# Last expert of a mixture-of-experts layer: weight conversions, the seventh expert's turns, a row gather and its sums each in an earlier step

## The chip, the cores and the metric

One core of a Trainium2 chip runs the whole program. The metric is the time of one execution on the device in microseconds (us). The engines are TensorE (PE), VectorE (DVE), ScalarE (ACT), GpSimd (POOL) and SyncE (SP). Each works through its own queue of instructions and waits on semaphores for the others. DMA transfers are issued here by SP (weights), ACT (rows of results) and POOL (gathers by index).

## What is computed

Attention with a local window, then a mixture of experts with the two best of eight experts per token, then a dense layer with the mish function. Only the second is around the change, and the first lines of the third.

```python
def _moe_ref(x, w_gate, w_noise, noise, w1, w2):
    ...
    for e in range(E):                       # 8 experts
        for k in range(2):
            mask = top2[:, k] == e
            h = np.maximum(x[mask] @ w1[e], 0.0)       # 512 -> 1024
            out[mask] += top2_w[mask, k, None] * (h @ w2[e])   # 1024 -> 512

def _moe2_ref(x, w_in, w_out):
    h = x @ w_in                             # 512 -> 2048
    sp = np.where(h > 20.0, h, np.log1p(np.exp(np.minimum(h, 20.0))))
    return ((h * np.tanh(sp)) @ w_out).astype(np.float32)
```

## The kernel before, in words

Every float32 product is made of three products of split operands (`three`, lines 858 to 860): high times high, high times low, low times high. So each operand exists as a high part, written by ACT, and a low part, written by DVE as the difference.

The experts run in 64 steps, `n = 8 * e + f`, with expert `e` and a block `f` of 128 of the 1024 hidden units. Each expert has up to 416 tokens (`CAP`). In a step:

- `first_layer(e, f)` makes 12 matmuls into a bank `hp`; ACT writes `hhi` (L904) and DVE `hlo` (L905) from it.
- `whole_layer` of the step before makes the second layer of the previous block, 12 matmuls from `hhi` and `hlo` into four banks `ac`. Its second matmul reads `hlo`.
- `w_split` splits the piece of expert weights that is needed two steps later: ACT writes `whi` (L277), DVE `wlo` (L280). `w_load` issues a load of 512 KB on SP (L265).
- In some steps `w64_begin` begins a conversion for the third layer, whose weights arrive as 64-bit words: four operations on DVE (L327 to L330). The last operations of a conversion, `half[4]`, stand in the next step: one on ACT (L322) and two on DVE (L323, L324). Below, "begin f" and "end f" are these two parts of the conversion that begins in step `f` of the last expert. `CONVS` lists the steps. `w64_load` issues the load of such a piece (512 KB, L301). All these loads share three buffers (`raw`), and a load waits until DVE has read the buffer's last content.
- In steps 1 to 4 of an expert, `turn_out` turns a quarter of the previous expert's result on PE (L934), ACT copies it to `ys` (L940) and stores it in `yd` (L941).

In the last expert (`e = 7`, steps `n` 56 to 63) there is more. `rest_rows` gathers six times 128 rows from `yd` on POOL (L1009), where the stores of all earlier experts have to be in; `rest_sum` weighs and adds each pair, on ACT (L1016) and DVE (L1017). Then comes `finish`: three quarters of the last block's second layer; `rest_turn`, which turns the sums on PE (L1024); copies of the four quarters of the result to `yT`, on ACT (L1038) and DVE (L1036); turns of these (L1043), the fourth quarter, and products that put the last expert's rows in their places (L1052). The third layer follows on PE.

The order of all this is the order in which the Python code issues it. On each engine the instructions stand in that order.

Of the kernel before, what the change touches and what calls it, by code (L numbers as in the profile page):

```python
# [20 lines left out]
NTOK, DM, E, F1, F2 = 1536, 512, 8, 1024, 2048  # L21
# [26 lines left out]
WEIGH = (3, 7)  # L48
ROOM = 2 * P + 3 * 2 * 32
CONV = (1, 3, 5)  # L50
CONVS = [8 * e + f for e in range(8) for f in CONV]
CONVS[0] = 7


# [122 lines left out]
def build(tc, ctx, I, out, n_global, n_local, dbg=None):  # L177
# [126 lines left out]
    def w64_begin():  # L304


        j, s = divmod(state["conv"], 2)
        if j == 16:
            return None
        state["conv"] += 1  # L310
        if s == 0:
            pool, n = (wlast, "l") if j < 16 - RING else (wring, "")
            pieces[64 + j] = (pool.tile([P, 1024], F32R, name="whi" + n), pool.tile([P, 1024], F32R, name="wlo" + n))
        raw = raws.pop((j, s))
        lw, uw = raw[:, :, 0], raw[:, :, 1]
        hi, lo = (w[:, s * 512:(s + 1) * 512] for w in pieces[64 + j])
        t1 = wtmp.tile([P, 512], I32, name="t1", bufs=2)
        t2 = wtmp.tile([P, 512], I32, name="t2", bufs=1)
        f1 = t1.bitcast(F32)

        def rest():
            A.activation(hi, f1, AF.Copy)  # L322
            V.tensor_tensor(f1, f1, hi.bitcast(F32), op=OP.subtract)  # L323
            V.tensor_tensor(lo, f1, lo.bitcast(F32), op=OP.add)  # L324

        return (
            lambda: V.tensor_scalar(t1, uw, 0x07FFFFFF, 3, op0=OP.bitwise_and, op1=OP.logical_shift_left),  # L327
            lambda: V.scalar_tensor_tensor(t1, uw, -0x40000000, t1, op0=OP.bitwise_and, op1=OP.bitwise_or),
            lambda: V.tensor_scalar(t2, t1, -0x800000, None, op0=OP.bitwise_and),
            lambda: V.scalar_tensor_tensor(lo, lw.bitcast(U32), 2.0 ** -52, t2.bitcast(F32), op0=OP.mult, op1=OP.mult),  # L330
            rest,
        )
# [3 lines left out]
    def gather(e, blocks=NT):  # L336
        for c, n in CHUNKS:
            k = e * 4 + c // P
            idx = (gidx if blocks == NT else gidx0)[:n, k:k + 1]
            xg = xg_p.tile([P, DM], F32, name="xg")  # L340
            G.indirect_dma_start(out=xg[:n], out_offset=None, in_=xd[:1 + blocks * P],
                                 in_offset=bass.IndirectOffsetOnAxis(ap=idx, axis=0))
            xgs[e, c] = xg
# [510 lines left out]
    ps_q = ctx.enter_context(tc.tile_pool(name="ps_q", bufs=1, space=PSUM))  # L854
# [30 lines left out]
    def turn_in(e, ci, pool, name):  # L885
        c, n = CHUNKS[ci]
        if ci == 0:
            xgT[e] = parts()
        xg = xgs.pop((e, c))
        tp = pool.tile([P, 4, P], F32, name=name)  # L890
        for d in range(4):
            T.transpose(tp[:, d, :n], xg[:n, d * P:(d + 1) * P], ident[:n, :n])  # L892
        split_ps(xgT[e][0][:, :, c:c + n], xgT[e][1][:, :, c:c + n], tp[:, :, :n])

    def first_layer(e, f):
        whi, wlo = (w.rearrange("p (d f) -> p d f", d=4) for w in pieces[8 * e + f // 2 * 2])
        xhi, xlo = xgT[e]
        c = (f % 2) * P
        hp = ps_h.tile([P, 512], F32, name="hp")
        for d in range(4):  # L900
            three(hp[:, :CAP], whi[:, d, c:c + P], wlo[:, d, c:c + P], xhi[:, d], xlo[:, d], d == 0, d == 3)
        hhi = mk.tile([P, CAP], F32R, name="hhi")
        hlo = mk.tile([P, CAP], F32R, name="hlo")
        A.activation(hhi, hp[:, :CAP], AF.Relu)  # L904
        V.scalar_tensor_tensor(hlo, hp[:, :CAP], 0.0, hhi.bitcast(F32), op0=OP.max, op1=OP.subtract)  # L905
        hT[e, f] = (hhi, hlo)
# [12 lines left out]
    def whole_layer(e, f):  # L919
        for _ in second_layer(e, f):  # L920
            pass
        if f == 7:
            yT[e] = mk.tile([P, 4, CAP], F32, name="yT", bufs=1)
            for d in range(4):
                if d % 2:
                    V.tensor_copy(yT[e][:, d], yps[e][d][:, :CAP])
                else:
                    A.activation(yT[e][:, d], yps[e][d][:, :CAP], AF.Copy)

    def turn_out(e, ci, pool, name):  # L930
        c, n = CHUNKS[ci]
        tp = pool.tile([P, 4, P], F32, name=name)
        for d in range(4):
            T.transpose(tp[:n, d], yT[e][:, d, c:c + n], ident)  # L934
        store_y(e, ci, tp)

    def store_y(e, ci, tp):
        c, n = CHUNKS[ci]
        ys = mk.tile([P, DM], F32, name="ys", bufs=3)
        A.activation(ys[:n], tp[:n].rearrange("p a b -> p (a b)"), AF.Copy)  # L940
        (nc.scalar if e + 1 < E else nc.sync).dma_start(yd[e * CAP + c:e * CAP + c + n, :], ys[:n])  # L941

    def some_places(t, n, name):

        ohr, ohc, ops = places_of(t, n, wlast.tile([P, 1024], F32R, name=name).bitcast(F32))
        for op in ops:
            op()
        return ohr, ohc

    def whole_list(parts):  # L950
        list_of(parts, ps_q.tile([P, 4, P], F32, name="tq").rearrange("p a b -> p (a b)")[:, :64])
# [36 lines left out]
    def places():  # L988

        oh = mk.tile([P, DM], F32, name="ys", bufs=3).rearrange("p (t s) -> p t s", s=P)  # L990
        for t in range(TC):
            V.tensor_scalar(oh[:, t], iot[:, :P], chi[:, t:t + 1], None, op0=OP.is_equal)
        ps = ps_q.tile([P, TC + 1, P], F32, name="tq")
        for t in range(TC):
            T.transpose(ps[:, t], oh[:, t], ident)
        for t in range(TC):
            T.matmul(ps[:, TC, :1], oh[:, t], wlh[:, 1, t:t + 1], start=(t == 0), stop=(t == TC - 1))
        V.tensor_copy(place, ps[:, :TC])
        V.tensor_copy(wslot, ps[:, TC, :1])

    def rest_rows():

        rl, rh = parts()
        got = []
        for t in range(TC):
            r = []
            for k, (w, idx) in enumerate(((rl, cidx[:, 0, t:t + 1]), (rh, crest[:, t:t + 1]))):
                y = w.rearrange("p a b -> p (a b)")[:, t * DM:(t + 1) * DM].bitcast(F32)
                G.indirect_dma_start(out=y, out_offset=None, in_=yd[:(E - 1) * CAP, :],  # L1009
                                     in_offset=bass.IndirectOffsetOnAxis(ap=idx, axis=0))  # L1010
                r.append(y)
            got.append(r)
        return got

    def rest_sum(t, r):
        A.activation(r[0], r[0], AF.Copy, scale=wlh[:, 0, t:t + 1])  # L1016
        V.scalar_tensor_tensor(r[1], r[1], wrest[:, t:t + 1], r[0], op0=OP.mult, op1=OP.add)  # L1017
# [80 lines left out]
    half = None  # L1098
    for n, (e, f) in enumerate(steps):
        if f == 0 and 0 < e < E - 1:  # L1100
            gather(e + 1)
        first_layer(e, f)
        if early and n < len(PARTS):
            lists.append(some_places(*PARTS[n]))
        if n == 1 and not early:
            gather(1)
        if 2 <= f <= 4 and e:
            turn_out(e - 1, f - 1, ps_q, "tq")
        if n == 7:
            turn_in(1, 3, ps_q, "tq")  # L1110
        if n:
            whole_layer(*steps[n - 1])
        if f == 1 and e:
            turn_out(e - 1, 0, ps_q, "tq")
        if n == LISTS and early:
            whole_list(lists)
            gather(1)
        if n == WEIGH[0]:
            weigh()
        if n == WEIGH[1]:  # L1120
            places()
        if (e, f) == (E - 1, 5):
            rest = rest_rows()
        if (e, f) == (E - 1, 7):
            for t in range(TC):
                rest_sum(t, rest[t])
        for ci in range(3 if e == 0 else 4):
            if f == (TURN if e == 0 else (3, 4, 5, 6))[ci] and e + 1 < E:
                turn_in(e + 1, ci, ps_q, "tq")
        conv = n in CONVS if n < 61 else True  # L1130

        if n + 1 in CONVS if n < 60 else True:
            w64_load()
        if n:
            w_split(A, V)
            w_load()
        if half:
            half[4]()
        half = w64_begin() if conv else None
        if half:  # L1140
            for op in half[:4]:
                op()
    half[4]()
    late = finish(rest)
    if "y" in dbg:
        nc.sync.dma_start(dbg["y"], yd[:7 * CAP])
# [99 lines left out]
    for n in range(len(steps) + 2):  # L1246
        new, old = n < len(steps), 1 <= n <= len(steps)
        if new:
            tb, f = steps[n]
# [3 lines left out]
        if n % 2 == 0:  # L1253
            half = w64_begin() if n else None
# [145 lines left out]
```

## Time and profile before

| | |
|---|---|
| median of 3 runs | 736.98 us (736.25 to 737.54) |
| the profiled execution | 739.06 us, of which 737.2 us from the first to the last instruction |
| PE busy | 708.8 us (96%) |
| DVE busy | 523.9 us (71%) |
| ACT busy | 424.0 us (58%) |
| mean granted TensorE clock | 0.986 of full speed |

The profiled execution took 2.1 us more than the median of the runs, 0.3%. The times within the trace are counted from the first instruction. The last expert's steps lie at about 390 to 428 us, `finish` at 428 to 442 us, and the third layer behind it.

### The profile page before, as it was taken

What the parts mean: (1) busy time and instruction counts of PE and PEld (TensorE: products, weight loads), DVE (VectorE), ACT (ScalarE), POOL (GpSimd) and SP (SyncE); (2) the same over time, 40 slices, a digit from 0 to 9 for tenths busy, and PEclk for the clock granted to TensorE, in tenths of its full rate; (3) what the DMA queues carried; (4) which work ended last, traced back from release to release, by engine and by line L of the source; (5) the groups of instructions that cost most, each with busy time, mean ns of one, the idle gap of its engine ahead of it and who ended that gap; (6) DMA issues with size and microseconds to landing.
All of it is one profiled execution on the core that took longest, in us unless ns stands there. A gap on an engine that the chain in (4) does not pass through costs nothing.

```text
span 737.2 us, 11732 instructions
## 1 busy us (share of the span) xinstructions
PE 708.8 (96%) x4259; PEld 643.7 (87%) x4259; DVE 523.9 (71%) x1237; ACT 424.0 (58%) x892; POOL 61.6 (8%) x83
## 2 busy tenths in 40 slices
PE   8999899999999999999999989898999999999995
PEld 4777779999999999999999978787999989989993
DVE  7789769977586676758575876888666666666663
ACT  5899632444444544444444437566667667667663
POOL 2000200301010100101000212100120020000000
PEclk9999899999999999999999999999999999999998
DMA  7799321757475655647454734300120030001001
GB/s 166 217 220 240 127 67 39 244 159 232 161 221 167 198 186 177 221 158 219 151 170 142 236 106 135 112 29 0 56 74 1 0 106 10 0 1 44 1 0 47
DMA packets 42932, 89.26 MB, mean 121 GB/s; under 512 B 5987, under 2 KB 18403, under 8 KB 42868
## 3 DMA queue, kind: packets, MB, share of 16 engines
q1 hardware_dynamic: 35412, 69.37, 31.4%
q0 software_dynamic: 4096, 13.11, 5.9%
q10 hardware_dynamic: 3360, 5.97, 2.1%
q8 instruction: 35, 0.57, 0.3%
q14 instruction: 29, 0.24, 0.1%
HBM read 75.32 MB, written 13.11 MB: 120 GB/s over the span
## 4 chain that ended last, share of the span: by engine, by line
PE 79%; DVE 10%; ACT 6%; DMA 2%; issue 1%; POOL 1%; ACTq 0%; DVEq 0%
PE hp L858 11%; PE hp L859 11%; PE hp L860 11%; PE ac L858 6%; PE ac L860 6%; PE ac L859 6%; PE ac L1225 5%; PE ac L1226 5%; PE ac L1230 4%; PE xp L567 3%; PE tp L554 2%; PE sp L516 2%; PE tq L892 2%; PE tq L934 2%; ACT r L1187 1%
## 5 line engine op out<-in xcount | busy, mean ns | idle before, releaser
L858 PE MATMUL hp<-xgh,whi 128*128 128x416 f32 (+1 forms) x288 | 104.2, 362 | 0.0
L280 DVE TENSOR_TENSOR wlo<-raw,whi 128x1024 fp32r<-128x1024 f32 x61 | 74.6, 1223 | 38.1 <-ACT whi L277 35.9
L859 PE MATMUL hp<-xgl,whi 128*128 128x416 f32 (+1 forms) x288 | 100.6, 349 | 0.2 <-DVE xgl L711 0.2
L860 PE MATMUL hp<-xgh,wlo 128*128 128x416 f32 (+1 forms) x288 | 100.7, 350 | 0.0
L858 PE MATMUL ac<-hhi,whi 128*128 128x416 f32 x256 | 92.0, 359 | 0.0
L859 PE MATMUL ac<-hlo,whi 128*128 128x416 f32 x256 | 90.1, 352 | 0.3 <-DVE hlo L905 0.3
L860 PE MATMUL ac<-hhi,wlo 128*128 128x416 f32 x256 | 90.1, 352 | 0.0
L1196 DVE SCALAR_TENSOR_TENSOR yT<-yT,r 128x384 f32<-128x384 f32 (+1 forms) x68 | 36.4, 535 | 73.9 <-ACT r L1191 69.9
L858 PE MATMUL hp<-xgh,whil 128*128 128x384 f32 x224 | 77.0, 344 | 0.0
L859 PE MATMUL hp<-xgl,whil 128*128 128x384 f32 x224 | 76.4, 341 | 0.0
L904 ACT ACTIVATE hhi<-hp 128x416 fp32r<-128x416 f32 x64 | 33.3, 520 | 74.7 <-PE hp L860 64.6
L860 PE MATMUL hp<-xgh,wlol 128*128 128x384 f32 x224 | 75.9, 339 | 0.0
L277 ACT ACTIVATE whi<-raw 128x1024 fp32r<-128x1024 f32 x61 | 64.4, 1055 | 17.2 <-PE ac L859 12.0
L1225 PE MATMUL ac<-whil,hhi 128*128 128x512 f32 x144 | 57.3, 398 | 1.5 <-ACT hhi L1201 1.3
L1226 PE MATMUL ac<-wlol,hhi 128*128 128x512 f32 x144 | 56.6, 393 | 0.0
L859 PEld LDWEIGHTS hp<-xgl,whi 128*128 128x128 f32 x288 | 54.3, 189 | 1.1 <-DVE xgl L711 0.4
L858 PEld LDWEIGHTS hp<-xgh,whi 128*128 128x128 f32 x288 | 54.2, 188 | 1.1 <-ACT xgh L710 0.4
L1181 ACT ACTIVATE yT<-hp 128x384 f32<-128x384 f32 (+1 forms) x68 | 31.6, 471 | 40.6 <-PE hp L860 37.4
L860 PEld LDWEIGHTS hp<-xgh,wlo 128*128 128x128 f32 x288 | 54.0, 188 | 0.4
L863 ACT ACTIVATE xgh<-tq 128x512 fp32r<-128x512 f32 (+2 forms) x38 | 20.2, 533 | 57.8 <-PE tq L892 57.8
L1201 ACT ACTIVATE hhi<-yT 128x384 fp32r<-128x384 f32 (+1 forms) x68 | 34.5, 507 | 31.7 <-DVE yT L1198 30.7
L905 DVE SCALAR_TENSOR_TENSOR hlo<-hp,hhi 128x416 fp32r<-128x416 f32 x64 | 37.5, 586 | 16.7 <-ACT hhi L904 16.7
(241 smaller groups left out, 1526.2 us busy)
## 6 DMA issues: line engine op xcount, KB each, us to landing
raw<-in_w_moe SPq DMA_DIRECT2D x96, 512.0 KB
yd<-ys ACTq DMA_DIRECT2D x21, 256.0 KB
ks<-in_k_t SPq DMA_DIRECT2D x24, 136.0 KB
qr<-in_q_t SPq DMA_DIRECT2D x24, 128.0 KB
vt<-in_v_w SPq DMA_DIRECT2D x12, 256.0 KB
xd<-xs SPq DMA_DIRECT2D x12, 256.0 KB
out<-ys SPq DMA_DIRECT2D x12, 256.0 KB
vt<-in_v_w SPq DMA_DIRECT2D x10, 208.0 KB
```

What stands on the lines that cost most here:

```text
L277: A.activation(hi, raw, AF.Copy)
L280: e_lo.tensor_tensor(lo, raw, hi.bitcast(F32), op=OP.subtract)
L858: T.matmul(ps, whi, xhi, start=first, stop=False)
L859: T.matmul(ps, whi, xlo, start=False, stop=False)
L860: T.matmul(ps, wlo, xhi, start=False, stop=last)
L904: A.activation(hhi, hp[:, :CAP], AF.Relu)
L905: V.scalar_tensor_tensor(hlo, hp[:, :CAP], 0.0, hhi.bitcast(F32), op0=OP.max, op1=OP.subtract)
L1181: A.activation(m[1][:, cc], m[0][:, cc], AF.Exp)
L1196: V.scalar_tensor_tensor(s, s, 1.0, r, op0=OP.add, op1=OP.mult)
L1201: A.activation(g[0][:, cc], m[1][:, cc], AF.Copy)
L1225: T.matmul(acc2[tb][c], ghi[:, cc], whi, start=(f == 0), stop=False)
L1226: T.matmul(acc2[tb][c], ghi[:, cc], wlo, start=False, stop=False)
```

## The change

The last expert's conversions begin in steps f = 1, 3, 4, 5, 6 instead of 1, 3, 5, 6, 7; nothing of a conversion is then left for after the last step. Their loads are issued a step earlier from the third of them on. The seventh expert's four turns stand in steps 1, 2, 3 and 3 (behind the second layer) instead of 1, 2, 3 and 4. The gathers stand in step 4 instead of 5 and the sums in step 6 instead of 7. The numbers of instructions stay the same.

```diff
-CONVS = [8 * e + f for e in range(8) for f in CONV]
+CONVS = [8 * e + f for e in range(7) for f in CONV] + [57, 59, 60, 61, 62]
...
-        if 2 <= f <= 4 and e:
+        if 2 <= f <= 4 and 0 < e < E - 1 or (e, f) == (E - 1, 2):
             turn_out(e - 1, f - 1, ps_q, "tq")
+        if (e, f) == (E - 1, 3):
+            turn_out(e - 1, 2, ps_q, "tq")
...
         if f == 1 and e:
             turn_out(e - 1, 0, ps_q, "tq")
+        if (e, f) == (E - 1, 3):
+            turn_out(e - 1, 3, ps_q, "tq")
...
-        if (e, f) == (E - 1, 5):
+        if (e, f) == (E - 1, 4):
             rest = rest_rows()
-        if (e, f) == (E - 1, 7):
+        if (e, f) == (E - 1, 6):
             for t in range(TC):
                 rest_sum(t, rest[t])
...
-        conv = n in CONVS if n < 61 else True
-
-        if n + 1 in CONVS if n < 60 else True:
+
+        if n + 1 in CONVS or n == 62:
             w64_load()
...
-        half = w64_begin() if conv else None
+        half = w64_begin() if n in CONVS else None
         if half:
             for op in half[:4]:
                 op()
-    half[4]()
     late = finish(rest)
```

On DVE, from the `hlo` of step 7 (the first row) to the first copy of `finish` (the last row), before:

```order
L905 SCALAR_TENSOR_TENSOR hlo<-hp,hhi 128x416
L1017 SCALAR_TENSOR_TENSOR xgl<-xgl,wrest,xgh 128x512 x3
L323 TENSOR_TENSOR t_5066<-t_5066,whil 128x512
L324 TENSOR_TENSOR wlol<-t_5066,wlol 128x512
L327 TENSOR_SCALAR t_5112<-raw 128x512
L328 SCALAR_TENSOR_TENSOR t_5112<-raw,t_5112 128x512
L329 TENSOR_SCALAR t_5113<-t_5112 128x512
L330 SCALAR_TENSOR_TENSOR wlol<-raw,t_5113 128x512
L323 TENSOR_TENSOR t_5112<-t_5112,whil 128x512
L324 TENSOR_TENSOR wlol<-t_5112,wlol 128x512
L1036 COPY yT<-ac 128x128
```

The same place in the change begins with the `hlo` of step 6; the `hlo` of step 7 is the second row L905:

```order
L905 SCALAR_TENSOR_TENSOR hlo<-hp,hhi 128x416
L1017 SCALAR_TENSOR_TENSOR xgl<-xgl,wrest,xgh 128x512 x3
L323 TENSOR_TENSOR t_5037<-t_5037,whil 128x512
L324 TENSOR_TENSOR wlol<-t_5037,wlol 128x512
L327 TENSOR_SCALAR t_5083<-raw 128x512
L328 SCALAR_TENSOR_TENSOR t_5083<-raw,t_5083 128x512
L329 TENSOR_SCALAR t_5084<-t_5083 128x512
L330 SCALAR_TENSOR_TENSOR wlol<-raw,t_5084 128x512
L905 SCALAR_TENSOR_TENSOR hlo<-hp,hhi 128x416
L323 TENSOR_TENSOR t_5083<-t_5083,whil 128x512
L324 TENSOR_TENSOR wlol<-t_5083,wlol 128x512
L1036 COPY yT<-ac 128x128
```

The three sums, the end of one conversion and the beginning of the next now stand ahead of the `hlo` of step 7, where before they stood behind it. Likewise begin 4 and begin 5 now stand ahead of the `hlo` of steps 5 and 6.

On ACT, in step 3, the difference begins behind the copy of the third turn (the first row):

```order
 L940 ACTIVATE ys<-tq 128x512
 L941 DMA yd<-ys 128x512
-L277 ACTIVATE whi<-raw 128x1024
-L904 ACTIVATE hhi<-hp 128x416
 L940 ACTIVATE ys<-tq 32x512
 L941 DMA yd<-ys 32x512
 L277 ACTIVATE whi<-raw 128x1024
```

The copy and the store of the fourth turn (32 rows) moved ahead of that step's split of weights.

## Rows read from the trace of the kernel before

**Rows 1.** Timeline of PE in `finish`: start, duration, instruction, [idle before, releaser].

```profile
430.36 0.49 PE L1024 MATMUL hp<-ident,xgl 128*128 128x128 f32 x2 [0.42 <-DVE xgl L1017]
431.70 1.83 PE L1024 MATMUL hp<-ident,xgl 128*128 128x128 f32 x14 [0.86 <-DVE xgl L1017]
435.23 0.33 PE L1043 MATMUL ac<-ident,yT 128*128 128x128 f32 x1 [1.02 <-ACT yT L1038]
436.81 0.41 PE L1043 MATMUL ac<-ident,yT 128*128 128x128 f32 x1 [1.26 <-DVE yT L1036]
```

**Rows 2.** Windows: us, busy of PE, PEld, DVE, ACT, POOL, granted clock, DMA.

```profile
437.00:440.40 3.40, 3.40 (x15) 3.25 (x15) 1.17 (x4) 0.86 (x2) 0.00 (x0) 0.51 0.02 5
```

**Rows 3.** Timeline of PE in the last expert.

```profile
409.28 0.35 PE L858 MATMUL hp<-xgh,whi 128*128 128x416 f32 x1
...
411.54 0.60 PE L934 MATMUL tq<-ident,yT 128*32 128x128 f32 x4
...
425.78 0.35 PE L859 MATMUL ac<-hlo,whi 128*128 128x416 f32 x1
...
428.04 0.36 PE L859 MATMUL ac<-hlo,whi 128*128 128x416 f32 x1
```

**Rows 4.** Timeline of DVE in the last expert.

```profile
409.31 1.23 DVE L280 TENSOR_TENSOR wlo<-raw,whi 128x1024 fp32r<-128x1024 f32 x1 [0.75 <-ACT whi L277]
...
415.53 1.23 DVE L280 TENSOR_TENSOR wlo<-raw,whi 128x1024 fp32r<-128x1024 f32 x1 [2.24 <-ACT whi L277]
416.67 0.68 DVE L323 TENSOR_TENSOR t<-t,whil 128x512 f32<-128x512 f32 x1
...
418.00 0.58 DVE L905 SCALAR_TENSOR_TENSOR hlo<-hp,hhi 128x416 fp32r<-128x416 f32 x1
418.50 1.22 DVE L280 TENSOR_TENSOR wlo<-raw,whi 128x1024 fp32r<-128x1024 f32 x1
419.63 0.42 DVE L327 TENSOR_SCALAR t<-raw 128x512 int32<-128x512 int32 x1
...
421.94 0.58 DVE L905 SCALAR_TENSOR_TENSOR hlo<-hp,hhi 128x416 fp32r<-128x416 f32 x1
...
426.40 0.59 DVE L905 SCALAR_TENSOR_TENSOR hlo<-hp,hhi 128x416 fp32r<-128x416 f32 x1 [0.24 <-ACT hhi L904]
...
430.90 0.75 DVE L1017 SCALAR_TENSOR_TENSOR xgl<-xgl,wrest,xgh 128x512 f32<-128x512 f32 x1 [0.60 <-ACT xgh L1016]
431.56 0.68 DVE L323 TENSOR_TENSOR t<-t,whil 128x512 f32<-128x512 f32 x1
```

**Rows 5.** Timeline of ACT in the last expert.

```profile
407.22 0.60 ACT L940 ACTIVATE ys<-tq 128x512 f32<-128x512 f32 x1
...
408.22 1.06 ACT L277 ACTIVATE whi<-raw 128x1024 fp32r<-128x1024 f32 x1 [0.40 <-ACT ys L940]
...
412.18 0.59 ACT L940 ACTIVATE ys<-tq 32x512 f32<-32x512 f32 x1
...
430.77 0.62 ACT L322 ACTIVATE whil<-t 128x512 fp32r<-128x512 f32 x1
```

**Rows 6.** The chain that ended last, 405 to 450 us: start, us, what.

```profile
412.82 5.05 DMA raw<-in_w_moe
...
417.88 1.03 POOL xgh L1009
```

**Rows 7.** DMA queues, 421 to 422.5 us: packets, MB, share (q1 SP, q0 gathers).

```profile
q1 hardware_dynamic: 78, 0.32, 74.8%
q0 software_dynamic: 13, 0.03, 4.9%
```

**Rows 8.** DMA queues, 412.8 to 417 us (q10 is ACT's stores).

```profile
q10 hardware_dynamic: 52, 0.07, 4.6%
```

**Rows 9.** Timeline of PE in the third layer, and the window (columns: busy of PE, clock, DMA) behind it.

```profile
473.91 0.66 PE L1162 MATMUL tq<-ident,ys 128*128 128x128 f32 x4 [3.17 <-DVE ys L1157]
474.50:475.00 0.50, 0.50 (x4) 0.50 0.00 0
```

## Prediction

> **What bounds the kernel now.** The page comes first: PE is busy for 96% of the span, so only the places where PE waits are worth reading, and a change that adds no PE work can give back at most what PE waits there. The waits of PE around the last expert come next, from its timeline [rows 1]. There are none in the eight steps, and four in `finish`: 0.42 and 0.86 us for the sums (L1017), 1.02 us for a copy by ACT, 1.26 us for a copy by DVE. Together 3.56 us. The reader is to see who stands behind them: DVE is late. It reaches the third sum at 430.90 [rows 4], because the gathered rows come late, and then still has two conversions ahead of its copies. Behind these waits the granted clock is 0.51 from 437.0 to 440.4 [rows 2], the lower of the two levels, 1.2 GHz. PE is busy for all of these 3.4 us, so at the upper level the same work would take 1.7 us. These two items, 3.56 us and up to 1.7 us, are all that the change can win.
>
> **What the change moves.** The counts stay; only the order on the engines changes. DVE's queue decides, so I lay its rows out anew. Distances between starts are the durations that count there: a split 1.14 us (415.53 to 416.67), the end of a conversion 1.33 (416.67 to 418.00), an `hlo` 0.50 (418.00 to 418.50, finished 0.58 after its start), the beginning of a conversion 2.31 (419.63 to 421.94), a sum 0.66 (430.90 to 431.56) [rows 4].
>
> Step 3: the fourth turn now stands on PE where the first layer of step 4 began, at 409.28 instead of 411.54 [rows 3], 2.26 us earlier. Its copy on ACT began 0.64 us after it (412.18 against 411.54), so at 409.92. The split on ACT that stood at 408.22 now stands behind it; from one such copy to the split behind it 1.00 us passed (407.22 to 408.22) [rows 5], so it starts at 410.92. DVE's part followed it by 1.09 us (409.31) [rows 4, 5], so at 412.01 instead of 409.31. DVE loses 2.7 us of work time, which costs nothing by itself: before, DVE sat idle for 2.24 us ahead of 415.53, waiting for the next split [rows 4]. That cover is used up now, and a conversion is added behind it.
>
> From 412.01 DVE has no idle time left. Its queue, with the starts: split 412.01, begin 3 413.15, `hlo` 4 415.46, split 415.96, end 3 417.10, begin 4 418.43, `hlo` 5 420.74, split 421.24, end 4 422.38, begin 5 423.71, `hlo` 6 426.02, three sums 426.52 to 428.50, end 5 428.50, begin 6 429.83, `hlo` 7 432.14. Only then come end 6 and the copies.
>
> When does PE want these? `hlo` 5 is there at 421.32; PE wants it a step (4.5 us) ahead of 425.78, at 421.2: a tenth, which I leave out. `hlo` 6 is there at 426.60 and wanted at 425.78 [rows 3]: a **wait of 0.8 us**. `hlo` 7 is wanted at 428.04 before [rows 3], so at 428.9 with that wait. By DVE's own work it is there at 432.72: a **wait of 3.8 us**, where before it began at 426.40, in time [rows 4]. PE's matmuls stay in program order here, so the turns of the sums cannot be done meanwhile. In return the four waits of [rows 1] go: when `hlo` 7 is there the sums are long done, and the last copy of DVE stands only 1.33 us behind it, while PE has three quarters of a second layer and 24 turns to do. So the lower bound is 0.8 + 3.8 - 3.56 = **+1.0 us**.
>
> **The gathers.** The sums now stand ahead of `hlo` 7, so a late gather holds up PE's matmuls. Let G be the start of the third sum; then `hlo` 7 is finished at G + 0.66 + 1.33 + 2.31 + 0.58 = G + 4.88. ACT is no way round: its L322 ran at 430.77 [rows 5], behind its sums. By DVE's own work G is 427.84. If the gathers land when they did before, G is 430.90 [rows 4], `hlo` 7 is there at 435.78, the wait is 6.9 us and the sum is 0.8 + 6.9 - 3.56 = **+4.1 us**, the upper bound. In between: POOL's first gather started at 417.88 [rows 6]. It needs the store of the fourth turn, whose packets (0.07 MB) ran until 417 [rows 8], and that store is issued 2.26 us earlier now. But the DMA engines get more to do at that time. A load of 512 KB is issued when DVE has freed its buffer. Between the store's old issue (about 412.8) and 423 there were four such loads (412.8, 416.7, 419.6, 421.9, each at the end of a split or a beginning). Now, between 413 and 423, there are five (413.2, 415.5, 417.1, 420.7, 422.4). At 0.32 MB in 1.5 us [rows 7] the fifth takes 2.4 us, as much as the store gains; about half of it can still fall behind the third pair of gathers, since the last load is issued no earlier than these. I take 2.26 - 1.0, thus G = 430.9 - 1.3 = 429.6, nearer to the old time than to 427.84. Then `hlo` 7 is there at 434.5, PE waits 5.6 us for it, and the sum is 0.8 + 5.6 - 3.56 = **+2.8 us**.
>
> **The clock.** A wait in one piece of 3.17 us in the third layer was followed by a granted clock of 0.50 [rows 9], as were the pieces in `finish` [rows 2]. The new wait is longer, so I expect the low stretch again, earlier and about as long: a difference of nothing, between -1.7 us (none) and some +1 us (it now falls on matmuls alone, where before some of it lay beside copies that PE would have waited for).
>
> **The rest.** The third layer is untouched, and all its conversions and loads are as far as before. The span of the profiled execution becomes 737.2 + 2.8 = 740.0 us and its time 741.9. It lay 2.1 us over the median of the runs, so for the median I add the same 2.8 us to 736.98: **739.8 us**, +0.4%. About 0.2% (1.5 us) is what a measurement of this kernel can tell from no change.
>
> **The rivals.**
>
> 1. *DVE's own work decides, because the gathers are early.* They need to land 2 us earlier than I take. By the Trainium skill, page "DMA: Bandwidth & Descriptors", section "Queues, rings and completion order", each DMA engine goes round robin between the queues that have work, a packet at a time, so the gathers would have an equal share beside the loads. If the gathers get half from the moment they are issued, the additional load delays them little and the store's 2.26 us and more reach the sums: +1.0 us, 738.0 us, no change that could be told. Against it: between 421 and 422.5, with two gathers issued, their queue moved 13 packets and the loads' 78 [rows 7]. By that rule the share should have been nearer to one half; the trace bears it out only in part. Chance 0.18.
> 2. *The gathers start no earlier, because a weight load holds them.* The chain has the load issued at 412.82 as what released POOL at 417.88 [rows 6]. The load in its place is now issued at 413.2, and with the same 5.05 us it lands at 418.2, 0.4 us later. Then G = 431.3 and the sum is +4.5 us: 741.5 us. For it speaks the chain; against it, that the store's last packets came just before that start as well [rows 8]. Chance 0.14.
> 3. *Not slower, by the clock.* The low clock does not come back: the wait in the second layer is short enough, and with the four small waits gone nothing else lowers it. Its price is 1.7 us, in `finish`, and it decides only if `hlo` 7 is there at 432.7, the lower bound: 738.0 - 1.7 = 736.3 us. Against it: even that wait, 3.8 us, is longer than the 3.17 us that lowered the clock in [rows 9]. Chance 0.08.
>
> **How the numbers follow.** My case, +2.8 us with G between 428.6 and 430.9 (738.8 to 741.1 us), has a chance of 0.60. The range takes in the first rival's 738.0 and the second's 741.5 with 0.3 us more on each side for the spread of the runs: 737.7 to 741.8. Left out are the third rival and tails of the others. Slower by over 0.2% is over 738.45: all of my case, the second rival and nothing of the others, 0.74. Within 0.2%: the first rival and half of the third, 0.21. Faster: what is left of the third and what I have not thought of, 0.05.
>
> **What the new profile would show.** Right: PE waits for DVE's `hlo` (L905) before two matmuls L859 into `ac`, under 1 us in step 7 and over 3.5 us at the head of `finish`, and the waits of [rows 1] are gone or small. DVE has no idle time between about 412 and the first sum. The first gather starts near 415. The clock falls once. Wrong: the `hlo` of step 7 finished before 430; or the splits of step 3 not delayed on ACT; or the sums so early that end 5 and begin 6 fit before 428; or a new wait of POOL that puts the gathers behind 418.

## The result, and the profile after

| | before | after | ratio, 95% interval |
|---|---|---|---|
| first measurement | 737.26 us (736.25 to 739.4, 6 runs) | 743.34 us (741.33 to 744.03, 6 runs) | 1.0080 (1.0057 to 1.0102) |
| second | 738.11 us (27 runs) | 741.69 us (739.36 to 743.99, 9 runs) | 1.0044 (1.0026 to 1.0063) |
| third | 737.01 us (10 runs) | 740.09 us (739.03 to 742.25, 6 runs) | 1.0049 (1.0033 to 1.0064) |

The change makes the kernel slower, as forecast, but the first measurement (+6.1 us between the medians, where +2.8 was forecast) lies outside the range. The two later measurements (+3.6 and +3.1 us) lie inside it. The profiled execution of the first measurement took 743.16 us.

Of the page of the changed kernel, the head, the busy times and the two groups of the second layer's matmuls that read `hlo` and `hhi` (columns: count, busy and mean ns, idle before and releaser):

```profile
span 741.4 us, 11732 instructions
...
PE 707.8 (95%) x4259; PEld 643.1 (87%) x4259; DVE 523.7 (71%) x1237; ACT 423.5 (57%) x892; POOL 61.8 (8%) x83
...
L859 PE MATMUL ac<-hlo,whi 128*128 128x416 f32 x256 | 90.8, 355 | 5.6 <-DVE hlo L905 5.6
L858 PE MATMUL ac<-hhi,whi 128*128 128x416 f32 x256 | 92.2, 360 | 0.0
```

The second of these groups on the page of before:

```profile
L859 PE MATMUL ac<-hlo,whi 128*128 128x416 f32 x256 | 90.1, 352 | 0.3 <-DVE hlo L905 0.3
```

No engine has more work: PE was busy for 708.8 us before. What grew is the idle time of PE, and the matmuls that read `hlo` have 5.6 us of it, where they had 0.3 us before.

The timeline of PE shows which two of the 256 these are, beside the first matmul of the experts and the first of the third layer:

```profile
110.50 0.46 PE L858 MATMUL hp<-xgh,whi 128*128 128x416 f32 x1
...
427.77 0.46 PE L859 MATMUL ac<-hlo,whi 128*128 128x416 f32 x1 [1.18 <-DVE hlo L905]
...
434.75 0.67 PE L859 MATMUL ac<-hlo,whi 128*128 128x416 f32 x1 [4.15 <-DVE hlo L905]
...
445.06 0.42 PE L858 MATMUL hp<-xgh,whil 128*128 128x384 f32 x1
```

The same two ends of the stage in the first trace of before:

```profile
110.00 0.45 PE L858 MATMUL hp<-xgh,whi 128*128 128x416 f32 x1
...
442.27 0.42 PE L858 MATMUL hp<-xgh,whil 128*128 128x384 f32 x1
```

The four waits of [rows 1] are gone, and two for `hlo` stand in their place, in step 7 and at the head of `finish`. Below, "the stage" is the time from the first matmul of the experts to the first of the third layer. It was 442.27 - 110.00 = 332.27 us before and is 445.06 - 110.50 = 334.56 us now, 2.3 us more.

DVE's timeline, which answers to [rows 4], and under it ACT's, which answers to [rows 5]:

```profile
412.48 1.23 DVE L280 TENSOR_TENSOR wlo<-raw,whi 128x1024 fp32r<-128x1024 f32 x1 [3.42 <-ACT whi L277]
...
424.88 0.43 DVE L327 TENSOR_SCALAR t<-raw 128x512 int32<-128x512 int32 x1 [0.69 <-DMA raw<-in_w_moe]
...
427.14 0.58 DVE L905 SCALAR_TENSOR_TENSOR hlo<-hp,hhi 128x416 fp32r<-128x416 f32 x1
427.64 1.41 DVE L1017 SCALAR_TENSOR_TENSOR xgl<-xgl,wrest,xgh 128x512 f32<-128x512 f32 x2
429.86 0.75 DVE L1017 SCALAR_TENSOR_TENSOR xgl<-xgl,wrest,xgh 128x512 f32<-128x512 f32 x1 [0.81 <-DMA xgl<-yd,crest]
430.53 0.68 DVE L323 TENSOR_TENSOR t<-t,whil 128x512 f32<-128x512 f32 x1
...
434.11 0.58 DVE L905 SCALAR_TENSOR_TENSOR hlo<-hp,hhi 128x416 fp32r<-128x416 f32 x1
```

```profile
410.40 0.59 ACT L940 ACTIVATE ys<-tq 32x512 f32<-32x512 f32 x1 [2.10 <-PE tq L934]
...
411.39 1.06 ACT L277 ACTIVATE whi<-raw 128x1024 fp32r<-128x1024 f32 x1 [0.40 <-ACT ys L940]
```

This is the predicted order at nearly the predicted times (this trace is 0.5 us late from the first expert on): ACT's split behind the fourth turn at 411.39 (410.92 was predicted), DVE's at 412.48 (412.01), the third sum at 429.86 (429.6), `hlo` 7 finished at 434.69 (434.5). What the reader is to see is the third sum's 0.81 us for gathered rows, and behind it everything that stands ahead of `hlo` 7.

### The profile page after: what moved, and what is told of

It reads as the page before. It is cut to its first block, busy times and chain, and to the rows that moved or that the text cites. A ratio compares the mean times of both kernels' runs of the same rounds, so it can differ in the third digit from the quotient of the medians.

```text
span 741.4 us, 11732 instructions
## 1 busy us (share of the span) xinstructions
PE 707.8 (95%) x4259; PEld 643.1 (87%) x4259; DVE 523.7 (71%) x1237; ACT 423.5 (57%) x892; POOL 61.8 (8%) x83
## 4 chain that ended last, share of the span: by engine, by line
PE 80%; DVE 10%; ACT 5%; issue 1%; DMA 1%; POOL 1%; another core or an unknown queue 0%; ACTq 0%; DVEq 0%
PE hp L858 11%; PE hp L859 11%; PE hp L860 11%; PE ac L859 6%; PE ac L860 6%; PE ac L858 6%; PE ac L1227 5%; PE ac L1228 5%; PE ac L1232 4%; PE sp L516 3%; PE tp L554 3%; PE xp L567 3%; PE tq L934 2%; PE tq L892 2%; ACT r L1189 1%
## 5 line engine op out<-in xcount | busy, mean ns | idle before, releaser
L859 PEld LDWEIGHTS ac<-hlo,whi 128*128 128x128 f32 x256 | 48.5, 189 | 7.4 <-DVE hlo L905 6.8
```

The costliest lines, as they stand in the source:

```text
L859: T.matmul(ps, whi, xlo, start=False, stop=False)
```

## The experiments

**The kernels again.** Both kernels were profiled three more times, since a single trace of each had carried the sum.

> The kernel before once more, to see how far executions of one kernel differ and where. Queue theory (the last expert's order on VectorE makes the whole difference): all executions within about 1 us, the third layer and the tail behind the last matmul as long as in the first trace of before (290.5 us from the first matmul of the third layer to the last, 6.4 us of tail). Rival (a part of the 6 us lies elsewhere: low-clock stretches in the third layer and the tail, which fall differently from execution to execution): the median is 1 to 2 us under the first profiled execution, and the third layer or the tail is shorter by that in this trace. Ratio 1.000 by both.

> The kernel before, a third profile. Clock theory: waits of 2.8 to 3.6 us in the last expert, and the low clock there in some executions only (one of two so far); with it the stage takes 332.3 us, without it 330.2. Rival (the low clock belongs to the kernel before, its absence was chance): low clock there again.

> The kernel before, a fourth profile. Clock theory: 2.6 to 3.6 us of waits in the last expert; without the low clock 330.0 to 330.3 us for the stage, with it 332.3. Rival: waits and stage outside of these two levels.

> The changed kernel once more, on the chip of these runs. Queue and clock theory (the hlo of steps 6 and 7 hold PE for some 5.3 us in pieces of 1.2 and 4.1, and a wait that long lowers the clock every time, where the waits of before lower it only in some executions): the same waits within 0.3 us, 3.4 us at the lower clock behind them again, and 334 to 335 us from the first matmul of the experts to the first of the third layer, against 330.2 in the last trace of before. 5 to 6 us over before. Rival (the low clock in the first trace of the change was chance, and the difference lies in the tail behind the last matmul): no low clock in this stage, about 332.8 us for it, and a tail of 9 us or more.

> The changed kernel, a third profile. Queue and clock theory: 4.3 to 5.6 us of waits for the hlo, the low clock for 3.4 us behind them, 333.2 to 334.7 us for the stage. Rival (the low clock is chance here too): no low clock, 331.5 to 333 us.

> The changed kernel a fourth time, against before in five rounds. Two measurements of the same kernel gave +0.8% (0.57 to 1.02) and +0.44% (0.26 to 0.63). Queue and clock theory (only the stage of the experts differs between the kernels, by 2.5 to 4.5 us in the traces so far; start and tail differ from execution to execution, whatever the kernel): 0.35 to 0.6%, stage 333.3 to 334.6 us, tail anywhere from 7.0 to 9.2 us. Rival (the change also lengthens the tail or the third layer): 0.7% or more, and a tail of 9 us or more again.

Before against itself gave 1.0010 (0.9996 to 1.0025). The 290.5 and 6.4 us that the expectation of `e0_before` names for the first trace are misread: its timeline has 287.9 us from the first matmul of the third layer to the end of the last, and 7.0 us behind it. `e0_before` has 288.0 and 7.9 us, so neither is shorter there; its median lies 1.1 us under the first profiled execution, and what is shorter is the stage, by 2.1 us. The times of `a0_after` and `a3_after` are the second and third measurement above; `a2_after`, a single profiled execution, took 740.47 us. From the four traces of each kernel (in the order first trace, then as listed; PE's waits from the last expert's steps to the end of `finish`; all in us):

| | waits of PE | mean | the stage | mean |
|---|---|---|---|---|
| before | 3.56, 2.76, 2.63, 2.65 | 2.90 | 332.27, 330.18, 330.05, 330.85 | 330.84 |
| after | 5.33, 4.33, 5.40, 4.42 | 4.87 | 334.56, 333.30, 334.43, 333.36 | 333.91 |

The first trace of before, on which the prediction rests, is the longest of its four. PE's waits in the last expert and `finish` of `e0_before` show what is usual: one wait of 0.48 us for the sums in place of 0.42 and 0.86, and the same two for copies:

```profile
431.18 1.83 PE L1024 MATMUL hp<-ident,xgl 128*128 128x128 f32 x14 [0.48 <-DVE xgl L1017]
...
434.70 0.33 PE L1043 MATMUL ac<-ident,yT 128*128 128x128 f32 x1 [1.02 <-ACT yT L1038]
...
436.30 0.33 PE L1043 MATMUL ac<-ident,yT 128*128 128x128 f32 x1 [1.26 <-DVE yT L1036]
```

The clock differs too. PE's windows (columns: us, busy of PE, granted clock, share of the DMA engines, GB/s) of `e0_before`, with no low clock:

```profile
432.00:436.00 4.00, 2.01 (x17) 1.00 0.00 0
436.00:440.00 4.00, 3.50 (x20) 1.00 0.02 4
```

and of the first trace of after:

```profile
432.00:436.00 4.00, 1.25 (x4) 0.85 0.00 0
436.00:440.00 4.00, 4.00 (x25) 0.72 0.00 0
```

A stretch of 3.4 us at the lower level, 1.2 GHz, stands behind the long wait in all four traces of after. In two of the four of before (the first and `b3_before`) such a stretch follows the short waits. The busy time of PE shows what it costs, since the stage has the same matmuls each time. The whole stage as one window, in the first trace of before, in `e0_before` and in the first trace of after (columns as above):

```profile
110.00:442.27 332.27, 327.51 (x1856) 0.99 0.56 178
110.53:440.71 330.18, 326.02 (x1857) 1.00 0.56 179
110.50:445.06 334.56, 327.83 (x1856) 0.99 0.56 176
```

PE was busy for 326.0 us in the two traces of before without the low stretch, 327.0 (`b3_before`) and 327.5 us in the two with it, and 327.6 to 327.8 us in all four of after: 1.0 us more on the mean. So the change adds about 2.0 us of waits (4.87 - 2.90), and 1.0 us of slower matmuls, because the low stretch now comes also in executions that had none. Together this is the 3.1 us by which the stage grew, and about what the second and third measurement show (+3.6 and +3.1 us).

Not all of the expectations held. For `a0_after` I had taken the first trace of after as usual (334 to 335 us of stage, 5 to 6 us over before); it has 333.30 us, and the measurement +3.6. And `b3_before` lies at neither of the two levels that I had expected (330.0 to 330.3, or 332.3 us): its low stretch cost 1.0 us, but its waits were no longer than usual. The first trace of before had both longer waits and a dearer stretch (1.5 us). The waits of `b2_before`, 2.63 us, lie a little under what I had expected (2.8 to 3.6).

**Which part costs.** From the change, the sums alone put back into step 7 (their old place, behind `hlo` 7):

```diff
-        if (e, f) == (E - 1, 6):
+        if (e, f) == (E - 1, 7):
             for t in range(TC):
                 rest_sum(t, rest[t])
```

> The changed kernel with its sums back in step 7, behind the hlo of step 7; all else as changed. Queue theory: the hlo of step 7 starts 2 to 3 us earlier, right behind begin 6 (near 431.3 instead of 434.1); PE waits 1.2 us for the hlo of step 6 and about 1.3 us for that of step 7 in place of 4.15, the turns of the sums do not wait, and the time is 3 to 5 us below the changed kernel, within 1.5 us of before. Rival (conversions alone are what holds the hlo, the sums are only carried along): the time stays within 1 us of the changed kernel, since the gathers land before the conversion would be done.

From before, the new conversion steps alone:

```diff
-CONVS = [8 * e + f for e in range(8) for f in CONV]
+CONVS = [8 * e + f for e in range(7) for f in CONV] + [57, 59, 60, 61, 62]
...
-        if n + 1 in CONVS if n < 60 else True:
+        if n + 1 in CONVS or n == 62:
...
-    half[4]()
```

> Before with the new steps of the conversions alone; turns, gathers and sums as before. Queue theory: the hlo of step 6 is late by about 0.3 us and that of step 7 by about 2 us, the sums and the copies then wait for nothing, so 2.4 us of waits in place of 3.56: before -1.2 us, 735.5 to 737. Rival (begin and end of a conversion ahead of the hlo cost as much as the whole change): 2 us or more over before.

From the change, the old conversion steps (that diff the other way round), so that turns, gathers and sums stay where the change has them:

> The change with the old steps of the conversions: turns, gathers and sums up by a step, one conversion still behind the last step. Queue theory: the sums and one conversion stand ahead of the hlo of step 7 as in the change, the hlo of step 6 is in time, and the copies wait for the last conversion: PE waits some 5 to 6 us for the hlo and 1 to 2 us for a copy, 2 to 4 us over before. Rival (the new steps of the conversions carry the cost): within 1 us of before.

| | ratio to before | median, us | the stage, us |
|---|---|---|---|
| `e1_sums7` | 0.9998 (0.9982 to 1.0013) | 736.36, before 736.97 | 329.37 |
| `e2_convonly` | 0.9971 (0.9957 to 0.9985) | 734.90, before 736.97 | 328.88 |
| `e3_oldconv` | 1.0059 (1.0037 to 1.0081) | 741.12, before 736.97 | 334.14 |

The first gives the whole loss back by one moved block of code. In DVE's timeline of `e1_sums7`, `hlo` 7 begins 3.6 us earlier than in after, counted from the first matmul of the experts (429.47 - 109.51 = 319.96, against 434.11 - 110.50 = 323.61). The three sums stand behind it and no longer wait for the gathers:

```profile
429.47 0.58 DVE L905 SCALAR_TENSOR_TENSOR hlo<-hp,hhi 128x416 fp32r<-128x416 f32 x1
429.97 2.06 DVE L1017 SCALAR_TENSOR_TENSOR xgl<-xgl,wrest,xgh 128x512 f32<-128x512 f32 x3
```

PE then waits 1.55 us for `hlo` 7 (and 0.40 us for `hlo` 6), as it does for `hlo` 7 in `e2_convonly`: that is begin 6, which the new steps put ahead of it. In return the waits for copies are gone, since no conversion begins behind the sums. So the new steps alone are faster, by 2.1 us; that was more than I had expected of them. In `e3_oldconv` the sums in step 6 wait longer for the gathers, since the old steps leave DVE free to reach them sooner and it then stands in front of the gathers for 1.86 and 2.02 us (DVE's timeline, then PE's):

```profile
429.21 0.75 DVE L1017 SCALAR_TENSOR_TENSOR xgl<-xgl,wrest,xgh 128x512 f32<-128x512 f32 x1 [2.02 <-DMA xgl<-yd,crest]
...
433.45 0.58 DVE L905 SCALAR_TENSOR_TENSOR hlo<-hp,hhi 128x416 fp32r<-128x416 f32 x1
```

```profile
434.09 0.72 PE L859 MATMUL ac<-hlo,whi 128*128 128x416 f32 x1 [4.36 <-DVE hlo L905]
```

Its wait for `hlo` 7 is as long as the change's, though the conversions are the old ones. I had also expected a wait for a copy there; there is none.

The sums have a part on ACT too, and in step 6 it stands ahead of ACT's `hhi` of step 7. In the first trace of after `hhi` is done at 430.08, and PE, which reads it at 430.13, shows no wait for it. In `e3_oldconv` and `f3_foursums6` PE waits 0.73 and 0.68 us for `hhi`, ahead of the long wait. `e1_sums7` moves both parts back.

**How much of it is the conversion between the sums and `hlo` 7.** From the change, the last conversion begun in step 7 instead of 6, which puts it behind `hlo` 7:

```diff
-CONVS = [8 * e + f for e in range(7) for f in CONV] + [57, 59, 60, 61, 62]
+CONVS = [8 * e + f for e in range(7) for f in CONV] + [57, 59, 60, 61, 63]
...
-        if n + 1 in CONVS or n == 62:
+        if n + 1 in CONVS or n == 63:
...
+    half[4]()
```

> The changed kernel with its last conversion in step 7 instead of 6, behind the hlo of step 7; its end stands behind the last step again. Queue theory: that hlo starts 2.3 us earlier (end 5 is all that stands between the third sum and it), PE's wait for it falls from 4.15 to about 1.9 us, a wait of 1 to 2 us for the copies by VectorE comes back, and the stage of the experts takes 331 to 332.5 us if the clock stays up: 2 to 3 us under the change. Rival (the late gathers hold the hlo, whatever stands behind them): 0 to 1 us under the change.

It measured 1.0002 (0.9984 to 1.0021). Its third sum begins at 430.00 and has waited 0.77 us for gathered rows, just as in after; but `hlo` 7 now follows 2.00 us behind it, not 4.25:

```profile
430.00 0.75 DVE L1017 SCALAR_TENSOR_TENSOR xgl<-xgl,wrest,xgh 128x512 f32<-128x512 f32 x1 [0.77 <-DMA xgl<-yd,crest]
...
432.00 0.58 DVE L905 SCALAR_TENSOR_TENSOR hlo<-hp,hhi 128x416 fp32r<-128x416 f32 x1
```

```profile
432.64 0.46 PE L859 MATMUL ac<-hlo,whi 128*128 128x416 f32 x1 [2.02 <-DVE hlo L905]
```

PE's wait is 2.02 us instead of 4.15, the clock stays at its upper level, the stage takes 330.69 us, and the loss is gone. The wait for the copies that I had expected did not come back. Against the first trace of after, whose gathers came as late, this prices the begun conversion: 2.1 us of wait, and with it the low clock.

**Less work for DVE.** Four conversions in the last expert instead of five (the fifth runs in the third layer), once with the sums back in step 7, once with nothing else of the change, once with the sums in step 6 as the change has them. All three have this line; `f1_four` also has the edit of `e1_sums7`, and `f2_fouronly`, made from before, the other lines of `e2_convonly`:

```diff
-CONVS = [8 * e + f for e in range(7) for f in CONV] + [57, 59, 60, 61, 62]
+CONVS = [8 * e + f for e in range(7) for f in CONV] + [57, 59, 61, 62]
```

> Turns and gathers up by a step as in the change, sums behind the hlo of step 7 as before, and the last expert with four conversions (steps 1, 3, 5, 6); the fifth moves into the third layer, where one more conversion begins in its step 14. Queue theory: both hlo are in time, sums and copies are there when PE comes to them, under 1 us of waits in the last expert, 327.5 to 328.5 us for the stage and 2 to 4 us under before. Rival (the third layer gives it back, since VectorE is busy there too): the stage is as short, but the third layer grows by 2 us or more, and the time is that of before.

> Before with four conversions in the last expert (steps 1, 3, 5, 6) and the fifth in the third layer; turns, gathers and sums as before. It parts what the last run with four conversions gained. Queue theory: the copies wait for nothing, the hlo of step 7 is in time, but the sums come when the gathers allow (near 430), so PE waits 0.3 to 1.3 us for them: 328.3 to 329.5 us for the stage, 0.5 to 1.5 us more than with the early gathers, and 1.5 to 3 us under before. Rival (the early gathers did it): within 1 us of before.

> The changed kernel with four conversions (steps 1, 3, 5, 6) and the sums in step 6 as in the change. Queue theory (what stands ahead of the hlo of step 7 behind the gathers decides, not how much VectorE has to do in all): the hlo of step 7 still waits for the third sum and a whole conversion, starts 4.3 us behind that sum (433 to 434 if the gathers land near 429) and holds PE for 4 to 5.5 us; 333 to 334.5 us for the stage, 3 to 5 us over before. Rival (VectorE's load decides): 3.6 us of work less, the hlo is in time or 1 us late, at or under before.

| | ratio to before | median, us | the stage, us |
|---|---|---|---|
| `f1_four` | 0.9955 (0.9942 to 0.9968) | 734.78, before 738.11 | 326.78 |
| `f2_fouronly` | 0.9956 (0.9942 to 0.9969) | 734.17, before 737.67 | 326.74 |
| `f3_foursums6` | 1.0048 (1.0034 to 1.0062) | 741.79, before 737.67 | 333.64 |

The third one settles whether DVE's load or its order costs. It has a whole conversion less (3.6 us of DVE's time), and is as slow as the change:

```profile
427.68 0.75 DVE L1017 SCALAR_TENSOR_TENSOR xgl<-xgl,wrest,xgh 128x512 f32<-128x512 f32 x1 [0.57 <-ACT xgh L1016]
...
431.93 0.58 DVE L905 SCALAR_TENSOR_TENSOR hlo<-hp,hhi 128x416 fp32r<-128x416 f32 x1
```

```profile
432.57 0.71 PE L859 MATMUL ac<-hlo,whi 128*128 128x416 f32 x1 [3.49 <-DVE hlo L905]
```

Between the third sum and `hlo` 7 stand the same 4.25 us as in after. `f1_four` differs from it in the place of the sums alone. With the sums behind `hlo` 7, the same four conversions leave PE without a single wait in the last expert and `finish`; DVE's timeline of `f1_four`:

```profile
427.29 0.58 DVE L905 SCALAR_TENSOR_TENSOR hlo<-hp,hhi 128x416 fp32r<-128x416 f32 x1
427.79 2.07 DVE L1017 SCALAR_TENSOR_TENSOR xgl<-xgl,wrest,xgh 128x512 f32<-128x512 f32 x3
...
431.10 0.65 DVE L1036 COPY yT<-ac 128x128 f32<-128x128 f32 x2
```

`f1_four` and `f2_fouronly` are faster than before by 0.4 to 0.5%. The two agree, so the earlier turns and gathers of `f1_four` buy nothing by themselves; I had expected `f2_fouronly` to wait for its sums, and it did not. The conversion moved to the third layer was hidden there in `f1_four`: from its first matmul to the end of the last took 287.9 us (286.1 to 288.0 in the four traces of before). In `f2_fouronly` it took 289.3.

## Why the prediction came out as it did

**Right: where the time goes.** The waits of [rows 1] gave way to two for `hlo`, under 1.2 us in step 7 and over 3.5 us at the head of `finish`, in all four traces. Of the causes, the experiments show two: the sums' place ahead of `hlo` 7 (`e1_sums7`, `f3_foursums6`) and the conversion begun between them (`g1_conv7`). The working from the third sum to `hlo` 7 (G + 4.88) measured 429.86 to 434.69, 4.83 us. In the step of the moved fourth turn one thing failed: "From 412.01 DVE has no idle time left". It waited 0.69 us for a weight load at 424.88, so `hlo` 6 began at 427.14, 1.1 us later than by the list (426.02), where the rows ahead of it were late by 0.4; its wait was 1.18 us instead of 0.8.

**The step that failed.** It is the last one of the sum: "It lay 2.1 us over the median of the runs, so for the median I add the same 2.8 us". It takes one trace of before as the usual execution, and the stage as the whole difference. Within the pair of traces that belong to the first measurement, the change cost 2.3 us of stage, near the 2.8. But the trace of before was long for a reason that belonged to the disputed place: its sums were late and its clock fell. In a usual execution there is less to give back, and on the mean of four traces of each kernel the stage grew by 3.1 us. Term by term, against these traces:

- *"5.6 us" for `hlo` 7 and 0.8 for `hlo` 6*: together 6.4 predicted, 4.87 measured. The wait for `hlo` 7 was 3.5 to 4.4 us. Two things made it shorter. In two of the four traces (`a0_after` and `a3_after`) the gathers were in time and the third sum waited for nothing; there the first gather began at 413.71 and 412.94, against 417.88 in the first trace of before. In the other two the third sum waited 0.81 us (the first, for rows) and 0.88 us (`a2_after`, put down to ACT). And PE itself came later to `hlo` 7, by 1.7 us in the first trace (430.60, where 428.9 was predicted), of which 0.5 is that trace's late start.
- *"Together 3.56 us" given back*: 2.90 on the mean, 2.63 to 2.76 in the three traces that I had not seen. Not typical, and too large by 0.7.
- *The clock, "a difference of nothing"*: the low stretch came in four of four traces of after and in two of four of before. PE was busy for 1.0 us more in the stage, the upper end of the bounds that the prediction gave ("some +1 us"). It gave a dearer stretch as the reason, and that is about 0.4 us of it: the stretch cost 1.0 and 1.5 us before and 1.6 to 1.8 after. The other 0.6 us come from the two executions of before that did not have it.

The first error made the forecast too high by 1.5 us, the other two too low by 0.7 and 1.0. That 2.8 came out close to the 3.1 us of the stage is luck: the errors cancel. It also means that these terms do not explain the first measurement. There the step fails by what it puts at nothing, all that lies outside the stage: 3.0 us of the 6.1 are not in the sum at all.

**What stays open.** The first measurement shows +6.1 us, and 3.0 us more than the stage's mean growth, and the cause of these is open. Between the two traces that belong to it, the spans differ by 4.2 us: the stage gave 2.3, its later start 0.5, the stretch behind the last matmul 2.2 (it took 9.2 us after and 7.0 before), and the third layer was 0.8 shorter. But that last stretch took 7.0 to 9.1 us in the four traces of before and 7.3 to 9.2 in those of after, so it varies by itself, and the third layer took 287.1 us in all four of after. The same changed kernel then gave +3.6 and +3.1 us. One number of the record points somewhere: the mean granted clock of the six runs was 0.981 to 0.985 (mean 0.9827), against 0.982 to 0.988 (0.9854) in the second measurement and 0.984 to 0.990 (0.9870) in the third. If PE was busy in that time, the difference is worth 2 to 3 us (an estimate: 0.0027 and 0.0043 of 741 us), the size of what is missing. But a longer stretch behind the last matmul lowers this mean too, since the granted clock there was 0.66 to 0.74 in the traces, and five of the six runs have no trace. So it is not shown where these 3.0 us lie, nor why the six runs had them.

**The rivals.** 1: the gathers were early in two of four traces, and the wait for `hlo` 7 was then 3.54 and 3.77 us against its 3.8. Its mechanism occurs; its time, 738.0 us, was too low, since it gave back the same 3.56 us and left the clock out. 2: refuted as a mechanism. POOL's first gather began at 412.94 to 415.62 in the four traces, before the 418.2 at which the load was to land. 3: refuted, the low clock came back in each of the four traces.

Rival 1 had the queues' shares at its root. In the first trace of after the gathers' queue (q0) moved more than the loads' (q1) from 422 to 424 us, and in `e0_before` less (columns: packets, MB, share of 16 engines):

```profile
q0 software_dynamic: 150, 0.50, 70.9%
q1 hardware_dynamic: 55, 0.20, 26.8%
```

```profile
q1 hardware_dynamic: 107, 0.40, 58.5%
q0 software_dynamic: 41, 0.16, 27.8%
```

So neither the 13 to 78 of [rows 7] nor an equal share holds for such a window; what decides the share of a queue in 2 us is not shown. The Trainium skill, page "DMA: Bandwidth & Descriptors", section "Queues, rings and completion order", says that an engine goes round robin between the queues that have work; the windows here don't contradict that, but they don't give the landing times by it either.

## What to carry to other kernels

An instruction that waits for a DMA, put ahead of one that makes a matmul's operand in the same engine's queue, passes its wait on to TensorE; what stands between the two (here the end of one conversion and the beginning of the next, 3.6 us) is added to it. Read the whole queue up to the operand, not only the load on the engine: with a conversion less, the same order was as slow. And where a change is worth less than 1%, as here, take the waits that it is to give back from several profiled executions, since one execution's waits can be the very thing that made it long.

## What the runs showed of the hardware

Every wait of 3.5 to 4.4 us in one piece came with the lower clock (six of six traces: four of after, `e3_oldconv`, `f3_foursums6`), but not always from the same moment. In the four of after it fell when the wait was over, for 3.4 us. In the other two, where a shorter wait of 0.7 us for `hhi` had come just ahead, it fell while PE was still waiting, and stayed low for 6.8 us. PE's windows of `f3_foursums6`, whose wait ended at 432.57:

```profile
430.00:430.50 0.50, 0.00 (x0) 0.94 0.00 0
430.50:431.00 0.50, 0.00 (x0) 0.50 0.00 0
...
436.00:437.00 1.00, 1.00 (x7) 0.50 0.00 0
437.00:437.50 0.50, 0.50 (x5) 0.74 0.00 0
```

It did not fall behind waits of 1.13 and 2.02 us (`g1_conv7`). Behind the three or four short waits of before, 2.6 to 3.6 us in sum, it fell in two executions of four: `b3_before` had the low stretch with waits of 2.65 us in sum, `b2_before` did not with 2.63. So the same kernel pays for it in some executions and not in others, and its own spread holds this.
